# Window attention, forward and backward: the y products ahead of the first window pair, and the weight gradient row between the pairs in 64x64 products

## The chip, the cores and the metric

One core of a Trainium2 chip runs the whole program. The metric is the device time of one execution in microseconds (us). Engines are named as in the profile: PE is TensorE (matmuls; PEld is its loading of stationary operands), DVE is VectorE, ACT is ScalarE, POOL is GpSimd, and SP is SyncE, which here only starts DMAs. PSUM, where matmuls leave their sums, has eight banks.

## The reference

Attention in windows of 8x8 tokens over an image of 256x256 tokens with 384 channels, without heads. The kernel computes the output and the gradients of `x`, `wqkv` and `wo` for a given `grad_out`, all in bfloat16.

```python
xw = x in windows: (1024, 64, 384)
q, k, v = split(xw @ wqkv, 3)
p = softmax((q @ k.T) * C ** -0.5)
o = (p @ v) @ wo
# outputs: o, and of sum(o * grad_out) the gradients by x, wqkv and wo
```

## The kernel before

The kernel never forms q, k and v. It folds the weights once at the start: `A` is Wq Wk^T with the scale, `B` is Wv Wo. With x and g (the rows of `grad_out`) of a window, the scores are x A x^T, the output is P (x B), and the gradient of P is (g B^T) x^T. The gradient by x is P^T (g B^T) + dS^T (x A) + dS (x A^T). For the weights it is enough to sum two 384x384 matrices over all windows, x^T (dS x) and x^T (P^T g); the code calls dS x `Uq`, P^T g `Wq`, and the two sums `GF_acc`. The gradients of the weights come from these sums at the very end (`weight_gradients`).

**Tiles.** Two windows that lie under each other make a tile of 128 tokens, one window in partitions 0 to 63 (`LO`), the other in 64 to 127 (`HI`). Four such tiles are a quad, and 128 quads are the image. A loop handles one quad a step, in a software pipeline of three stages: in step i the quad i+1 is in stage A, quad i in stage B and quad i-1 in stage C.

**Stages.** Stage A is two projections of 3 row blocks each (`project`, L149): kind 0 makes z = B g^T, kind 1 makes y = A^T x^T, nine products of 512 columns each; ACT evicts them to `yz` (L159, L161). `gather` (L163), on DVE, copies z or y once more into `zy`, which a transposing DMA on SP's queue turns into `tok` (`to_tokens`, L169). Stage B makes the scores and the gradient of P (`scores`), the softmax and its backward in six pieces on DVE and ACT (`soft`), and x B and x A^T (`uv`, L227: eight banks, evicted by ACT at L235). Stage C is `attend` (L249), once for the tiles 0 and 1, and once for 2 and 3: a pair. Between them, and ahead of the first, `filler` (L326) takes work from `gf_group` (L311).

**attend.** All its products are 64x64: one window's 64 tokens are the rows, and the stationary operand has 64 columns. A slot (L257) is four such products with 384 moving columns: a straight one for each half, which leaves its result in its own half of the partitions, and a crossed one for each half, which leaves it in the other half. A pair is six slots. It uses eight PSUM tiles: two `pw`, two `pu`, two `po` (one each per token tile, straight) and two `pd` (crossed, accumulated over the slots). In the order in which they are first written: slot 1 takes `pw` and both `pd`, slot 2 `pw`, slot 3 `pu`, slot 4 `po`, slot 5 `pu`, slot 6 `po`. Slot by slot they are evicted: `pw` of the first tile by ACT (L281), `pw` of the second by DVE (L283), both `pu` by DVE (L285, L289), both `po` by ACT (L270), the first `pd` by ACT (L270), the second in halves (L296 on ACT, L297 on DVE for the first pair and on ACT for the second). Then POOL starts the stores (L298 to L305).

**gf_group.** When three quads are finished, their contribution to `GF_acc` is added: two matrices (f) of three row blocks (ma) make six rows. A row is twelve full 128x128 products (3 quads times 4 tiles) that accumulate in one PSUM tile `pg` (L320), and one DVE addition into `GF_acc` (L321). `filler(1)` makes one row; it is called twice in a step.

**Order.** The order of each engine's instructions is the order of the calls; nothing is reordered. All PSUM tiles come from one ring of eight banks, in the order of their first writes: a tile gets the bank whose last reader stands earliest, and PE waits for that reader. In the allocation of the kernel before, for instance, slot 6 of the first pair gets the bank of the `pg` ahead of it. One step (L334) allots 33 tiles: 1 for the scores, 8 for `uv`, 3 for z, 1 `pg`, 8 for the first pair, 3 for y, 1 `pg`, 8 for the second pair. On PE a step is therefore: scores, `uv`, z, row, pair, y, row, pair. On DVE, from the first row on: the addition, L283, L285, L289, L297, gather of z, gather of y, the addition, L283, L285, L289. On ACT: z, pair, y, pair. On SP's queue, in order: the turns of g and x for the quad after next (`load_turn`, L129), the turn of P and dS (`turn`), four loads of x, the turn of `zy`.

Of the kernel before, what the change touches and what calls it, by code (L numbers as in the profile page):

```python
# [9 lines left out]
ALU = mybir.AluOpType  # L10
AX = mybir.AxisListType
BF16 = mybir.dt.bfloat16
F32 = mybir.dt.float32

P = 128
WIN = 8
WT = WIN * WIN
QUAD = 4
# [4 lines left out]
def kernel(  # L23
# [21 lines left out]
    nc = tc.nc  # L45
    _, H, W, C = x.shape
# [10 lines left out]
    ring = ctx.enter_context(tc.tile_pool(name="ring", bufs=8, space=bass.MemoryType.PSUM))  # L57
# [11 lines left out]
    GF_acc = const.tile([P, 2, CK, C], F32)  # L69
# [41 lines left out]
    def weight_rest():  # L111
        weight_product(B_sb, wT[2], wo_sb, None)
        weight_product(AT_sb, wT[1], wT[0], scale)

    def windows(ap, st, first, count=2):
        row, col = st["at"]
        return ap[0, row + WIN * first:row + WIN * (first + count), col:col + WIN, :]

    LO, HI = slice(0, WT), slice(WT, P)
    OTHER = {0: HI, WT: LO}  # L120

    def load(st):
        st["xq"] = xq = grp.tile([P, QUAD, C], BF16, tag="xq", name="xq", bufs=2 * GQ + 4)
        st["dq"] = dq = qp.tile([P, QUAD, C], BF16, tag="dq", name="dq", bufs=6)
        for t in range(QUAD):
            nc.sync.dma_start(out=xq[:, t, :], in_=windows(x, st, 2 * t))
            nc.gpsimd.dma_start(out=dq[:, t, :], in_=windows(grad_out, st, 2 * t))  # L127
# [16 lines left out]
    def product(out, lhsT, rhs, start, stop):  # L144
        nc.tensor.matmul(out, lhsT=lhsT, rhs=rhs, start=start, stop=stop)  # L145
# [37 lines left out]
    def over_k(ap, n=P):  # L183
        return ap.unsqueeze(2).broadcast_to([n, QUAD, WT])

    def soft(st, step):
        sd = st["sd"]
        if step == 0:
# [53 lines left out]
    def operand(st, n, t, h):  # L242
        if n in ("PT", "ST"):
            return st["PS"][h, t, int((n == "ST") == (h == LO)), :]
        if n in ("z", "y"):
            return st["tok"][h, int(n == "y"), :, t, :]
        return st[n][h, t, :]

    def attend(st, pair):  # L249
        if pair[0] == 0:  # L250
            st["Uq"] = grp.tile([P, QUAD, C], BF16, tag="Uq", name="Uq")
            st["Wq"] = grp.tile([P, QUAD, C], BF16, tag="Wq", name="Wq")

        def bank(name):
            return ring.tile([P, C], F32, tag="r", name=name)

        def slot(straight, crossed, start=False, stop=False):  # L257
            for h in (LO, HI):
                dst, lhs, rhs, t = straight
                products = [(h, dst[h, :], lhs, rhs, t, {"start": True, "stop": True})]  # L260
                lhs, rhs, t = crossed
                o = OTHER[h.start]
                dst = pd[int((t == t0) == (h == LO))]
                products.append((o, dst[o, :], lhs, rhs, t, {"start": start, "stop": stop}))
                for o, dst, lhs, rhs, t, flags in products if h == LO else products[::-1]:
                    nc.tensor.matmul(dst, lhsT=operand(st, lhs, t, h), rhs=operand(st, rhs, t, h), **flags)  # L266

        def keep(name, src):
            sb = ob.tile([P, C], BF16, tag=name, name=name)
            nc.scalar.copy(out=sb[:], in_=src[:])  # L270
            return sb

        t0, t1 = pair
        pw = {t: bank("pw") for t in pair}
        pu = {t0: bank("pu")}
        pd = [bank("pd") for outer in (0, 1)]
        po = {t0: bank("po")}
        pu[t1] = bank("pu")
        po[t1] = bank("po")
        slot((pw[t0], "Pb", "dq", t0), ("Pb", "z", t0), start=True)  # L280
        nc.scalar.copy(out=st["Wq"][:, t0, :], in_=pw[t0][:])  # L281
        slot((pw[t1], "Pb", "dq", t1), ("dS", "y", t0))
        nc.vector.tensor_copy(out=st["Wq"][:, t1, :], in_=pw[t1][:])  # L283
        slot((pu[t0], "ST", "xq", t0), ("Pb", "z", t1), start=True)
        nc.vector.tensor_copy(out=st["Uq"][:, t0, :], in_=pu[t0][:])  # L285
        slot((po[t0], "PT", "uq", t0), ("dS", "y", t1))
        o0 = keep("o", po[t0])
        slot((pu[t1], "ST", "xq", t1), ("ST", "vq", t0), stop=True)
        nc.vector.tensor_copy(out=st["Uq"][:, t1, :], in_=pu[t1][:])  # L289
        slot((po[t1], "PT", "uq", t1), ("ST", "vq", t1), stop=True)  # L290
        o1 = keep("o", po[t1])
        inner = keep("d", pd[0])
        if t0 == 0:
            st["mid"], st["rim"] = [ob.tile([P, C], BF16, tag="d", name="d") for k in range(2)]
        upper, lower = (st["rim"], st["mid"]) if t0 == 0 else (st["mid"], st["rim"])
        nc.scalar.copy(out=lower[LO, :], in_=pd[1][LO, :])  # L296
        (nc.scalar.copy if t0 else nc.vector.tensor_copy)(out=upper[HI, :], in_=pd[1][HI, :])  # L297
        nc.gpsimd.dma_start(out=windows(out_0, st, 2 * t0), in_=o0[:])  # L298
        nc.gpsimd.dma_start(out=windows(out_0, st, 2 * t1), in_=o1[:])
        nc.gpsimd.dma_start(out=windows(out_1, st, 2 * t0 + 1), in_=inner[:])  # L300
        if t0 == 0:
            nc.gpsimd.dma_start(out=windows(out_1, st, 0, 1), in_=st["rim"][HI, :])
        else:
            nc.gpsimd.dma_start(out=windows(out_1, st, 3), in_=st["mid"][:])
            nc.gpsimd.dma_start(out=windows(out_1, st, 7, 1), in_=st["rim"][LO, :])  # L305

    fill = []

    final = {}

    def gf_group(sts, last=False):  # L311
        n = len(sts) * QUAD
        for f in range(2):
            if last:
                final[f] = grp.tile([P, CK, C], BF16, tag="Uq", name="GFb")
            for ma in range(CK):
                pw = ring.tile([P, C], F32, tag="r", name="pg")
                for i in range(n):
                    st, t = sts[i // QUAD], i % QUAD
                    product(pw[:], st["xq"][:, t, ma * P:(ma + 1) * P], st["UW"[f] + "q"][:, t, :], i == 0, i == n - 1)  # L320
                nc.vector.tensor_tensor(out=GF_acc[:, f, ma, :], in0=pw[:], in1=GF_acc[:, f, ma, :], op=ALU.add)  # L321
                if last:
                    nc.vector.tensor_copy(out=final[f][:, ma, :], in_=GF_acc[:, f, ma, :])
                yield

    def filler(n):  # L326
        while n and fill:
            try:
                next(fill[0])
                n -= 1  # L330
            except StopIteration:
                fill.pop(0)

    def step(c, b, a, ahead):  # L334


        def on(st):
            return (lambda f, *r: f(st, *r)) if st is not None else (lambda f, *r: None)
        C_, B, A = on(c), on(b), on(a)
        B(scores)  # L340
        B(soft, 0)
        if b is not None and c is None:
            weight_rest()
        B(uv, 0, 0)
        B(uv, 0, 1)
        B(soft, 1)
        B(uv, 1, 0)
        B(uv, 1, 1)
        B(soft, 2)
        B(soft, 3)  # L350
        B(uv, 2, 0)
        B(uv, 2, 1)
        B(uv, 3, 0)
        B(uv, 3, 1)
        B(soft, 4)
        for mo in range(CK):
            A(project, 0, mo)
        B(soft, 5)
        B(turn)
        if ahead is not None:  # L360
            load(ahead)
        filler(1)
        C_(attend, (0, 1))
        A(gather, 0)
        for mo in range(CK):
            A(project, 1, mo)
        A(gather, 1)
        A(to_tokens)
        filler(1)
        C_(attend, (2, 3))  # L370

    G_ON_PE, X_ON_PE = 4, 1
    EV = {"z": "AAA", "y": "AAA", "u": "AAAA", "v": "AAAA", "o": "AAAA", "U": "DDDD", "W": "DDDD", "d": "AAAA"}
    quads = [(row, col) for row in range(0, H, 2 * WIN * QUAD) for col in range(0, W, WIN)]
    sts = [{"at": q, "i": i} for i, q in enumerate(quads)]
    n = len(sts)
# [41 lines left out]
    with tc.manual_schedule(engines=MANUAL):  # L418
# [19 lines left out]
        for i in range(-1, n + 1):  # L438
            if 0 <= i < n - 2:
                load_turn(sts[i + 2])  # L440
            step(get(i - 1), get(i), get(i + 1), get(i + AHEAD) if i >= 0 else None)
            if 0 < i + 2 < G_ON_PE:
                turn_on_pe(sts[i + 2], "dq", "dT")
            if i == 1:
                turn_blocks(woT_sb, wo_sb)
            if i > 0:
                held.append(sts[i - 1])
                sts[i - 1] = None
            if held and i == n:
                last = gf_group(held, True)  # L450
            elif len(held) == GQ:
                fill.append(gf_group(held))
                held = []
        filler(1 << 30)
        weight_gradients(last)

# [29 lines left out]
```

## Time and profile before

| | us |
|---|---|
| median of 3 runs | 1943.18 |
| lowest, highest | 1942.42, 1948.91 |
| the profiled execution (span) | 1942.8 |
| PE busy | 1926.6 |
| ACT busy | 1546.3 |
| DVE busy | 1458.9 |
| POOL busy | 895.2 |

A line of the groups or of a timeline names the source line, the engine, the operation, the tiles written and read, the shape, and how many instructions it stands for; in a timeline the first two numbers are the start and the time until the last of them ended. In brackets stands how long the engine had been idle before, and what it waited for. Consecutive instructions on one engine overlap a little, so their durations can add up to more than the time that they took together: twelve products of 384 columns have 326 ns each, and take 2.11 us. Durations of one, in ns: a 128x128 product with 384 columns 326, a 64x64 one 318 to 348, the addition into `GF_acc` 558, a cast of 384 columns out of PSUM 548 on DVE and 473 to 500 on ACT, an eviction of z or y 607 to 644, a `gather` copy 560.

### The profile page before, as it was taken

How to read it: one execution, taken by the hardware profiler on the slowest of the kernel's cores; microseconds unless marked ns; L12 is line 12 of the kernel's file. 1: busy time of each engine (PE TensorE's matmuls, PEld its weight loads, DVE VectorE, ACT ScalarE, POOL GpSimd, SP SyncE). 2: the span in 40 equal slices, each digit the busy share in tenths (PEclk: the TensorE clock that was granted, in tenths of full speed). 3: DMA queues.
4: the chain of work that ended last, by engine and by line, in shares of the span. 5: the costliest groups of instructions: out<-in, count | busy, mean ns of one | idle time of the engine just before them, and what ended most of it. 6: DMA issues, size and time to landing. Idle time of an engine off the chain costs nothing.

```text
span 1942.8 us, 48771 instructions
## 1 busy us (share of the span) xinstructions
PE 1926.6 (99%) x17859; PEld 1076.9 (55%) x17859; DVE 1458.9 (75%) x3244; ACT 1546.3 (80%) x3613; POOL 895.2 (46%) x1670
## 2 busy tenths in 40 slices
PE   9999999999999999999999999999999999999999
PEld 5555555555555555555555555555555555555555
DVE  6777767777777777777777777777777777777776
ACT  7878878778777878887787878788887878887775
POOL 3445444444444445444444454454444445444432
PEclk9999999999999999999999999999999999999999
DMA  8999999999999999999999999999999999999994
GB/s 186 220 222 227 224 204 222 224 217 224 223 221 226 226 220 223 226 221 220 219 228 222 221 219 229 221 225 217 230 218 228 224 219 220 226 224 219 222 195 109
DMA packets 1017584, 423.21 MB, mean 218 GB/s; under 512 B 899584, under 2 KB 992768, under 8 KB 1017344
## 3 DMA queue, kind: packets, MB, share of 16 engines
q1 hardware_dynamic: 935984, 267.85, 79.0%
q0 software_dynamic: 79872, 151.17, 30.8%
q8 instruction: 140, 2.29, 0.5%
q10 hardware_dynamic: 1488, 1.08, 0.2%
q14 instruction: 100, 0.82, 0.1%
HBM read 101.84 MB, written 101.84 MB: 105 GB/s over the span
## 4 chain that ended last, share of the span: by engine, by line
PE 94%; ACT 2%; DMA 2%; DVE 1%; issue 0%; SPq 0%; POOL 0%; ACTq 0%; POOLq 0%
PE pj L145 49%; PE pg L145 25%; PE pw L266 6%; PE sd L145 5%; PE pu L266 4%; PE po L266 4%; DMA PS<-ps 1%; DMA dT<-dq 1%; PE pd L266 1%; ACT uq L235 0%; ACT vq L235 0%; DMA dq<-in_grad_out_dram 0%; ACT yz L159 0%; PE pe L385 0%; SPq L134 0%
## 5 line engine op out<-in xcount | busy, mean ns | idle before, releaser
L298 POOL DMA_DIRECT2D out_dram<-o x256 | 137.7, 538 | 936.8 <-ACT o L270 915.8
L145 PEld LDWEIGHTS <-xq 128*128 128x128 bf16 x3072 | 300.0, 98 | 226.4 <-issue 2.0
L145 PEld LDWEIGHTS <-xT 128*128 128x128 bf16 x3072 | 291.6, 98 | 182.7
L145 PE MATMUL pj<-B_sb,xT 128*128 128x384 bf16 x1536 | 333.5, 326 | 0.0
L145 PE MATMUL pj<-AT_sb,xT 128*128 128x384 bf16 x1536 | 333.3, 326 | 0.0
L127 POOL DMA_DIRECT2D dq<-in_grad_out_dram x512 | 271.9, 547 | 40.4 <-DMA out_dram<-o 17.6
L281 ACT CAST Wq<-pw 128x384 bf16<-128x384 f32 x256 | 123.0, 480 | 200.1 <-PE pw L266 200.0
L145 PE MATMUL pj<-dT,BT_sb 128*128 128x512 bf16 x1152 | 271.3, 381 | 5.1 <-DMA dT<-dq 5.1
L145 PE MATMUL pg<-Uq,xq 128*128 128x384 bf16 x1536 | 270.4, 326 | 0.5 <-DVE GF_acc L321 0.5
L145 PE MATMUL pj<-xT,A_sb 128*128 128x512 bf16 x1152 | 270.8, 380 | 0.0
L145 PE MATMUL pg<-Wq,xq 128*128 128x384 bf16 x1536 | 270.4, 326 | 0.0
L321 DVE TENSOR_TENSOR GF_acc<-pg,GF_acc 128x384 f32<-128x384 f32 x258 | 143.9, 558 | 152.8 <-PE pg L145 152.7
L235 ACT CAST uq<-pj 128x384 bf16<-128x384 f32 x512 | 249.9, 488 | 7.3 <-PE pj L145 1.0
L235 ACT CAST vq<-pj 128x384 bf16<-128x384 f32 x512 | 255.1, 498 | 0.1
L270 ACT CAST o<-po 128x384 bf16<-128x384 f32 x512 | 220.9, 484 | 5.1 <-PE po L266 2.4
L211 ACT COPY ps<-Pb 64x256 bf16<-64x256 bf16 x256 | 103.2, 403 | 149.7 <-DVE Pb L208 148.2
L159 ACT CAST yz<-pj 128x512 bf16<-128x512 f32 x384 | 206.7, 644 | 2.1 <-PE pj L145 2.0
L161 ACT CAST yz<-pj 128x512 bf16<-128x512 f32 x384 | 200.8, 607 | 0.2
L145 PEld LDWEIGHTS <-BT_sb 128*128 128x128 bf16 x1152 | 112.4, 98 | 129.8 <-DMA dT<-dq 7.0
L145 PEld LDWEIGHTS <-A_sb 128*128 128x128 bf16 x1152 | 102.3, 98 | 139.9 <-issue 33.6
L167 DVE COPY zy<-yz 128x1536 bf16<-128x1536 bf16 x256 | 143.4, 560 | 46.3 <-ACT yz L161 39.8
L266 PE MATMUL pd<-tok,Pb 64*64 64x384 bf16 x1024 | 173.3, 335 | 0.0
(89 smaller groups left out, 3376.1 us busy)
## 6 DMA issues: line engine op xcount, KB each, us to landing
xq<-in_x_dram SPq DMA_DIRECT2D x512, 96.0 KB, 4.2
dq<-in_grad_out_dram POOLq DMA_DIRECT2D x512, 96.0 KB, 4.0
out_dram<-o POOLq DMA_DIRECT2D x512, 96.0 KB, 4.0
out_dram<-d POOLq DMA_DIRECT2D x384, 96.0 KB, 4.2
out_dram<-d POOLq DMA_DIRECT2D x256, 48.0 KB, 4.3
tok<-zy SPq DMA_TRANSPOSE x128, 7.6
PS<-ps SPq DMA_TRANSPOSE x128, 4.7
xT<-xq SPq DMA_TRANSPOSE x127, 6.3
```

What stands on the lines that cost most here:

```text
L127: nc.gpsimd.dma_start(out=dq[:, t, :], in_=windows(grad_out, st, 2 * t))
L145: nc.tensor.matmul(out, lhsT=lhsT, rhs=rhs, start=start, stop=stop)
L159: ENG[EV["z"][mo]](out=yz[:, mo, :, 0:4:3, :], in_=pj[:])
L161: ENG[EV["y"][mo]](out=yz[:, mo, :, 1:3, :], in_=pj[:])
L167: nc.vector.tensor_copy(out=st["zy"][:, kind, :, :, :, :], in_=src)
L211: nc.scalar.copy(out=ps[h, :, w, :], in_=Pb[h, :, :])
L235: cp(out=dst[:, t, :], in_=pj[:])
L266: nc.tensor.matmul(dst, lhsT=operand(st, lhs, t, h), rhs=operand(st, rhs, t, h), **flags)
L270: nc.scalar.copy(out=sb[:], in_=src[:])
L281: nc.scalar.copy(out=st["Wq"][:, t0, :], in_=pw[t0][:])
L298: nc.gpsimd.dma_start(out=windows(out_0, st, 2 * t0), in_=o0[:])
L321: nc.vector.tensor_tensor(out=GF_acc[:, f, ma, :], in0=pw[:], in1=GF_acc[:, f, ma, :], op=ALU.add)
```

## The change

Three edits. First, in `step`, the four calls that make y (with both gathers and `to_tokens`) move ahead of the first pair, and the first `filler(1)` goes behind them. PE's order becomes: scores, `uv`, z, y, row, pair, row, pair. On DVE both gathers then stand ahead of the first row's addition and of the first pair's casts; on ACT the y evictions stand directly behind those of z. Second, the row between the pairs (in steps that have a quad in stage C) is made by `gf_rows_tiled`: in place of a 128x128 product four 64x64 ones, two for each half of the tokens, each into its own half of the output's rows. The straight ones accumulate in one bank, the crossed ones in another, and DVE adds both to `GF_acc`, one after the other. A step thus allots 34 PSUM tiles. Third, for the second pair the cast of the second `pw` (L283) goes from DVE to ACT.

```diff
-        nc.vector.tensor_copy(out=st["Wq"][:, t1, :], in_=pw[t1][:])
+        (nc.scalar.copy if t0 else nc.vector.tensor_copy)(out=st["Wq"][:, t1, :], in_=pw[t1][:])
...
+    def gf_rows(sts, f, ma):
+        pw = ring.tile([P, C], F32, tag="r", name="pg")
+        n = len(sts) * QUAD
+        for i in range(n):
+            st, t = sts[i // QUAD], i % QUAD
+            product(pw[:], st["xq"][:, t, ma * P:(ma + 1) * P], st["UW"[f] + "q"][:, t, :], i == 0, i == n - 1)
+        return [pw]
+
+    def gf_rows_tiled(sts, f, ma):
+        straight, crossed = [ring.tile([P, C], F32, tag="r", name="pg") for k in range(2)]
+        n = len(sts) * QUAD
+        for i in range(n):
+            st, t = sts[i // QUAD], i % QUAD
+            for h in (LO, HI):
+                products = ((h, straight), (OTHER[h.start], crossed))
+                for o, dst in products if h == LO else products[::-1]:
+                    nc.tensor.matmul(dst[o, :], lhsT=st["xq"][h, t, ma * P + o.start:ma * P + o.stop],
+                                     rhs=st["UW"[f] + "q"][h, t, :], start=(i == 0), stop=(i == n - 1))
+        return [straight, crossed]
+
     def gf_group(sts, last=False):
-        n = len(sts) * QUAD
...
-                pw = ring.tile([P, C], F32, tag="r", name="pg")
-                for i in range(n):
-                    st, t = sts[i // QUAD], i % QUAD
-                    product(pw[:], st["xq"][:, t, ma * P:(ma + 1) * P], st["UW"[f] + "q"][:, t, :], i == 0, i == n - 1)
-                nc.vector.tensor_tensor(out=GF_acc[:, f, ma, :], in0=pw[:], in1=GF_acc[:, f, ma, :], op=ALU.add)
+                for pw in (gf_rows_tiled if tiled[0] else gf_rows)(sts, f, ma):
+                    nc.vector.tensor_tensor(out=GF_acc[:, f, ma, :], in0=pw[:], in1=GF_acc[:, f, ma, :], op=ALU.add)
...
-    def filler(n):
+    def filler(n, in_tiles=False):
+        tiled[0] = in_tiles
...
-        filler(1)
-        C_(attend, (0, 1))
         A(gather, 0)
         for mo in range(CK):
             A(project, 1, mo)
         A(gather, 1)
         A(to_tokens)
         filler(1)
+        C_(attend, (0, 1))
+        filler(1, c is not None)
         C_(attend, (2, 3))
```

More of the change, by code (lines that the diff above doesn't have):

```diff
@@ L307 @@
     fill = []
+    tiled = [False]
     final = {}
+    def gf_rows(sts, f, ma):
[16 more added lines that the diff above has]
+        return [straight, crossed]
     def gf_group(sts, last=False):
-        n = len(sts) * QUAD
         for f in range(2):
```

## The prediction

> **What bounds the kernel now.** I read the head of the page and its chain first, then the timeline of one step in the middle of the run, then the groups by shape for the mean durations.
>
> ```profile
> PE 1926.6 (99%) x17859; PEld 1076.9 (55%) x17859; DVE 1458.9 (75%) x3244; ACT 1546.3 (80%) x3613; POOL 895.2 (46%) x1670
> ...
> PE 94%; ACT 2%; DMA 2%; DVE 1%; issue 0%; SPq 0%; POOL 0%; ACTq 0%; POOLq 0%
> ```
>
> PE is the chain: nearly nothing ever makes it wait. So a step costs what PE's instructions cost, plus what the other engines newly make PE wait. In the trace the steps start (first `sd` product to first `sd` product) 14.80 us apart, almost without scatter. One step, in parts (the columns: start, duration, engine, line, operation):
>
> ```profile
> 1001.05 2.11 PE L145 MATMUL pg<-Wq,xq 128*128 128x384 bf16 x12
> 1003.10 0.35 PE L266 MATMUL pw<-dq,Pb 64*64 64x384 bf16 x1
> ...
> 1003.45 0.32 PE L266 MATMUL pu<-xq,PS 64*64 64x384 bf16 x1
> ...
> 1003.61 0.32 PE L266 MATMUL po<-uq,PS 64*64 64x384 bf16 x1
> ...
> 1003.94 0.32 PE L266 MATMUL po<-uq,PS 64*64 64x384 bf16 x1
> ...
> 1004.20 2.12 PE L145 MATMUL pj<-xT,A_sb 128*128 128x512 bf16 x9
> ```
>
> What to see: a slot of four 64x64 products starts every 0.16 us (1003.45, 1003.61), which is also what one 128x128 product takes (12 in 2.11, the last 0.33 long: 0.162 each). At the borders between the two shapes there is more: the last `pg` product starts at 1002.83 and the first slot 0.27 later instead of 0.16; that slot takes 0.18 to 0.19 instead of 0.16; and the last slot starts at 1003.94 and `pj` 0.26 later. Going in and out costs 0.10 + 0.02 + 0.10 = 0.22 us, twice in a step.
>
> ```profile
> 1008.30 0.56 DVE L321 TENSOR_TENSOR GF_acc<-pg,GF_acc 128x384 f32<-128x384 f32 x1 [0.67 <-PE pg L145]
> ...
> 1008.78 0.55 DVE L283 CAST Wq<-pw 128x384 bf16<-128x384 f32 x1
> ...
> 1009.03 0.32 PE L266 MATMUL po<-uq,PS 64*64 64x384 bf16 x1
> ...
> 1009.09 0.86 ACT L270 CAST o<-po 128x384 bf16<-128x384 f32 x2
> ...
> 1009.30 0.87 PE L145 MATMUL sd<-xT,yz 128*128 128x64 bf16 x24
> ...
> 1016.75 1.61 ACT L159 CAST yz<-pj 128x512 bf16<-128x512 f32 x3
> ```
>
> What to see here: the bank of `pg` is read by VectorE until 1008.86, and the sixth slot, which needs the last of the eight banks, starts at 1009.03. All eight banks are claimed by the eight tiles of a pair, and the margin is 0.17 us. And ScalarE evicts the `z` products, which PE began at 1013.91, only from 1016.75: it is late there because its `uq` and `vq` casts wait for the softmax chain.
>
> ```profile
> 1005.48 1.56 ACT L161 CAST yz<-pj 128x512 bf16<-128x512 f32 x3
> ...
> 1007.07 0.56 DVE L167 COPY zy<-yz 128x1536 bf16<-128x1536 bf16 x1 [0.30 <-ACT yz L161]
> ```
>
> The second `gather` copy waits for the last `y` eviction, and starts 0.03 after it.
>
> **The change, part by part**, in us per step; it acts on 125 steps (42 groups of six rows are drained two per step, from the fifth step with a finished quad on; the two left over are made at the end, untiled).
>
> *Switches, -0.22.* With `y` ahead of the pair and the row between the pairs in 64x64 shape, PE goes into that shape and out of it once in a step instead of twice. Nothing else changes in PE's work: twelve 128x128 products of 0.162 become twelve slots of four 64x64 products at 0.162, 1.95 us both times. No row shows twelve such slots in a sequence into two banks; the nearest is the pair itself, whose later slots keep 0.16 with accumulating and overwriting products mixed. I take that value. Bounds: no gain, since no row shows 384 columns in less than 0.16, and +1.95 if the slots ran at half the rate (two pairs of products after each other).
>
> The Trainium skill (TensorE: Matmul & The Clock Gate, section LDWEIGHTS) gives a weight load its column count over 1.2 GHz, and four loads of 64 columns would then be 213 ns in a slot, above 162. By that rule the twelve slots would take 2.56 us, some 76 us more in the run. The pair's slots start four loads of 107 ns each and still come every 162 ns, so here the row decides.
>
> *Banks of the second pair, +0.55.* I put zero at the first product of the second pair (1008.19 now). A pair takes eight banks; six come from the first pair, and the two that are left are those of the tiled row, since the pair's own first bank is read until 0.89 (1008.60 plus 0.48, less 1008.19). The last tiled slot starts at -0.16 and its products end at 0.16; VectorE starts 0.04 later (1008.30 now, after an end of 1008.26) and adds for 0.56, to 0.76; slot 5 wants that bank at 0.65 and gets it at 0.79. The second add reads and writes the same slice of `GF_acc`; I let it start as dependent VectorE work does in the trace, 0.03 after the end: 0.79 to 1.35. Slot 6 starts at 1.38 instead of 0.84. The scores start 0.27 later, at 1.65 (now 1.10): +0.55. If the second add overlaps the first as L283 does L321 (0.48 apart, 1008.30 and 1008.78) this is 0.43; with hand-overs to PE of 0.07, 0.62. The L283 cast that goes to ScalarE (0.37 apart in a run of such casts) is free there: the second `o` cast behind it waits for slot 6 anyway. If slot 6 weren't late, that queue would be 0.37 later.
>
> *VectorE behind the gather, +0.24.* The second `o` cast, now at 1.27, starts at 1.76, and all that ScalarE does behind it, up to the `z` evictions, is 0.49 later: 9.05 instead of 8.56. The `y` evictions no longer stand behind the first pair's casts but directly behind the `z` ones: three casts 0.48 apart put them at 10.50, and 1.56 more ends them at 12.06. The gather waits for this, 12.09 to 12.65, and on VectorE the add of the first `pg` row and the L283 cast now stand behind the gather: the add runs from 12.68 to 13.24. PE meanwhile: scores 1.65, `z` 4.62 later, `y` 1.95, `pg` 1.95, and in at 12.20 (1.95 + 0.09 on); slot 6 would start at 13.03, and needs the bank of `pg`: 13.27. Bounds: 0, if ScalarE comes 0.25 earlier; 0.45, if it comes that much later.
>
> *The bank of the crossed products, +0.31.* The tiled row is next, at 13.43. Its straight bank is that of the first `pw` (read to 13.1 by ScalarE), its crossed one that of the second `pw`, whose cast (L283) starts 0.48 behind the add, at 13.16, and ends at 13.71: 13.74. Were VectorE not late at all, the cast would still end 1.13 after the pair began, as it does now (1003.68 + 0.55 - 1003.10), and the row wants the bank at 1.00: the low end is 0.15, the high one 0.40. Twelve slots later, at 15.69, the second pair begins; now it is 14.80.
>
> *Queues.* SP issues the same in the same order: the turn of `zy` stays behind the loads, and is some 7 us late already (issued at 1014.97 for a gather that ended at 1007.63). The `xT` turn issued at 1007.33 lands 6.3 later, at 1013.6; the `y` products that read it start 9.7 after the scores now (1019.0), 6.6 then (1015.9). So 2.3 us are left; in the steps where SP is later than this PE would wait, as now for `dT` (the groups show 5.1 us on PE and 7.0 on its weight loads in the whole run): 0 to 12, taken as 0. POOL's order stays; its stores follow the casts.
>
> Sum: -0.22 + 0.55 + 0.24 + 0.31 = 0.88; times 125, 110. The profiled execution spans 1942.8, so 2053; the median of the runs, 1943.18, is 0.4 above that span, which I leave out.
>
> **The rivals.**
> *Only the waits that the number of banks forces* (chance 0.15): the adds overlap, ScalarE is early enough for the gather: 0.43 + 0.15 - 0.22 = 0.36, times 125: 1988. For it: 0.24 hangs on ScalarE's lateness, which I carried over eight microseconds. Against: the `o` cast is tied to slot 6.
> *The switches alone* (0.05): the banks come free in time, 127 steps gain 0.22: 1915. This needs the sixth slot of the second pair served by 0.81, that is both adds over within 0.65 of the row's end, where with the hand-over two take 1.1 to 1.2 by the rows. It decides only if banks are handed out otherwise than I think. Somewhere between, within 0.3%: 0.03.
> *Half rate in the tiled row* (0.05): 1.95 more in each step on top of the forecast, 244: 2297. For it speaks that both banks take products from both row halves at once. Against it: so does the bank of `pw`, `pu` and `po` now, at full rate.
> The Trainium skill (TensorEngine Tiling, Gotcha 1) says that different row tiles can't access one bank at the same time, which taken literally would be this rival. The pair's slots show no such cost where the halves go to different partitions.
>
> **How the numbers follow.** The forecast, bank waits with a late VectorE, has 0.72, and gives 2053. The low end is the first rival's 1988; the high end takes the upper bounds, 0.62 + 0.45 + 0.40 - 0.22 = 1.25 or 156: 2099, of which I keep 2090, since all of them together are unlikely. 0.3% is 6 us, about what a measurement of this kernel can tell from no change. Slower: 0.72 + 0.15 + 0.05 = 0.92; same 0.03; faster 0.05.
>
> **What the profile after would show.** PE's share falls to some 94%, with idle time before `pu` and `po` of the second pair put down to VectorE's adds (L321's successor), before `po` of the first pair put down to the same line, and before the first crossed product put down to L283. Steps 15.5 to 15.8 apart. One PE weight-load gap of 0.3 (into the shape) in a step instead of two. Tiled slots 0.16 apart. It would be wrong if PE showed no idle time at the sixth slot, or if tiled slots were more than 0.2 apart.

## The result and the profile after

The changed kernel takes 2040.38 us (median of 4, 2034.85 to 2042.81) where the kernel before takes 1942.80: slower by the factor 1.0497 (95% interval 1.0471 to 1.0522). The profiled execution spans 2041.0, 98.2 more than that of before. In the trace the steps are 15.545 us apart (median over 100 steps, first scores product to first scores product) where they were 14.796. 0.749 more, times the 123 steps from the fifth on, is 92 of the 98 us; most of the rest is in steps that wait for a transfer.

The head of the page after and its chain:

```profile
span 2041.0 us, 58149 instructions
...
PE 1979.9 (97%) x22359; PEld 1164.0 (57%) x22359; DVE 1469.2 (72%) x3241; ACT 1605.5 (79%) x3741; POOL 893.6 (44%) x1670
...
ACT 44%; PE 19%; issue 12%; DVE 11%; DMA 9%; POOL 3%; SPq 0%; POOLq 0%; ACTq 0%
```

The busy share of PE hardly moved, from 99% to 97%, and would mislead. The chain tells it: before, 94% of the way back from the end went over PE; now 44% of it goes over ScalarE's casts, 11% over VectorE (the gather and the addition among others) and 19% over PE. PE's share stays high because a product is recorded as 0.32 us long where the next could have started after 0.16, so the first 0.16 of every wait hides under the product ahead of it (the 0.46 below is recorded as 0.28 idle).

One step of the changed kernel, in its timeline (start, duration, engine, line, operation; idle time before and its releaser in brackets). First, what happens around the first pair:

```profile
960.15 1.65 ACT L161 CAST yz<-pj 128x512 bf16<-128x512 f32 x3
...
961.83 0.56 DVE L167 COPY zy<-yz 128x1536 bf16<-128x1536 bf16 x1 [0.91 <-ACT yz L161]
...
962.42 0.32 PE L266 MATMUL pu<-xq,PS 64*64 64x384 bf16 x1
...
962.42 0.56 DVE L338 TENSOR_TENSOR GF_acc<-pg,GF_acc 128x384 f32<-128x384 f32 x1
...
962.90 0.55 DVE L283 CAST Wq<-pw 128x384 bf16<-128x384 f32 x1
963.04 0.32 PE L266 MATMUL po<-uq,PS 64*64 64x384 bf16 x1 [0.28 <-DVE GF_acc L338]
...
963.20 2.44 PE L328 MATMUL pg<-Wq,xq 64*64 64x384 bf16 x48
```

The `y` evictions end at 961.80, the gather follows at 961.83, the addition at 962.42, done at 962.98, and only at 963.04 can the sixth slot (`po`) start, 0.62 after the fifth where 0.16 would do: 0.46 lost. The addition itself could have started at 961.85, just after its products ended (961.81). In the kernel before it did start that early, 0.10 after the first product of its pair (1003.10):

```profile
1003.20 0.56 DVE L321 TENSOR_TENSOR GF_acc<-pg,GF_acc 128x384 f32<-128x384 f32 x1 [0.46 <-PE pg L145]
```

In the changed kernel the 48 products of the 64x64 row take 2.44 instead of the 2.1 of twelve slots: they begin at 963.20 on the straight bank, and the second of them, on the crossed bank, starts only at 963.50, behind the L283 cast that ends at 963.45. That is another 0.30. Then the second pair:

```profile
965.68 1.15 DVE L338 TENSOR_TENSOR GF_acc<-pg,GF_acc 128x384 f32<-128x384 f32 x2 [0.43 <-PE pg L328]
...
965.81 0.32 PE L266 MATMUL po<-uq,PS 64*64 64x384 bf16 x1
965.84 0.48 ACT L281 CAST Wq<-pw 128x384 bf16<-128x384 f32 x1 [1.18 <-PE pw L266]
...
965.97 0.32 PE L266 MATMUL po<-uq,PS 64*64 64x384 bf16 x1
...
966.29 0.32 PE L266 MATMUL pu<-xq,PS 64*64 64x384 bf16 x1
...
966.46 0.32 PE L266 MATMUL po<-uq,PS 64*64 64x384 bf16 x1
...
966.76 0.86 PE L145 MATMUL sd<-xT,yz 128*128 128x64 bf16 x24
```

The first of the two additions runs from 965.68 to 966.24, and `pu` of slot 5 starts at 966.29, 0.32 after the last product of slot 4 (965.97): 0.17 lost. `po` of slot 6 then starts 0.16 later, while the second addition, which ends at 966.83, is still running. It waits for nothing.

So, against the step before: -0.22 for the changes of shape, +0.46, +0.30 and +0.17 for three waits. That makes 0.71 of the 0.749; most of the rest is some 0.02 to 0.03 each time that PE starts again after a wait, when three of the four products of the first slot are recorded with 0.35 and the slot takes 0.18 to 0.19.

### The profile page after: what moved, and what is told of

Its sections match the earlier page's. It is cut to its first block, busy times and chain, and to the rows that moved or that the text cites. A ratio compares the mean times of both kernels' runs of the same rounds, so it can differ in the third digit from the quotient of the medians.

```text
span 2041.0 us, 58149 instructions
## 1 busy us (share of the span) xinstructions
PE 1979.9 (97%) x22359; PEld 1164.0 (57%) x22359; DVE 1469.2 (72%) x3241; ACT 1605.5 (79%) x3741; POOL 893.6 (44%) x1670
## 4 chain that ended last, share of the span: by engine, by line
ACT 44%; PE 19%; issue 12%; DVE 11%; DMA 9%; POOL 3%; SPq 0%; POOLq 0%; ACTq 0%
PE pg L328 11%; ACT vq L235 8%; ACT yz L161 7%; ACT yz L159 7%; ACT uq L235 7%; ACT o L270 4%; DMA xT<-xq 3%; DVE GF_acc L338 3%; DVE zy L167 3%; ACT d L297 2%; DVE Pb L208 2%; DVE rs L204 2%; ACT ps L211 2%; ACT ex L200 2%; PE pj L145 2%
## 5 line engine op out<-in xcount | busy, mean ns | idle before, releaser
L338 DVE TENSOR_TENSOR GF_acc<-pg,GF_acc 128x384 f32<-128x384 f32 x383 | 213.6, 558 | 73.5 <-PE pg L328 52.1
L270 ACT CAST o<-po 128x384 bf16<-128x384 f32 x512 | 234.3, 493 | 36.9 <-PE po L266 33.6
L328 PEld LDWEIGHTS <-xq 64*64 64x64 bf16 x6000 | 213.4, 106 | 63.5 <-issue 38.4
L266 PE MATMUL po<-uq,PS 64*64 64x384 bf16 x1024 | 194.9, 325 | 32.6 <-DVE GF_acc L338 31.6
L145 PEld LDWEIGHTS <-xq 128*128 128x128 bf16 x1572 | 153.6, 98 | 114.9 <-issue 0.5
L161 ACT CAST yz<-pj 128x512 bf16<-128x512 f32 x384 | 211.6, 673 | 3.6 <-PE pj L145 2.7
L266 PEld LDWEIGHTS <-PS 64*64 64x64 bf16 x3072 | 138.2, 105 | 130.1 <-issue 107.1
L159 ACT CAST yz<-pj 128x512 bf16<-128x512 f32 x384 | 206.0, 640 | 0.3 <-PE pj L145 0.2
L328 PE MATMUL pg<-Wq,xq 64*64 64x384 bf16 x3984 | 202.0, 324 | 0.0
L145 PEld LDWEIGHTS <-A_sb 128*128 128x128 bf16 x1152 | 111.7, 98 | 149.6 <-DVE ps L223 6.5
```

Of the source, the lines that this page charges most:

```text
L159: ENG[EV["z"][mo]](out=yz[:, mo, :, 0:4:3, :], in_=pj[:])
L161: ENG[EV["y"][mo]](out=yz[:, mo, :, 1:3, :], in_=pj[:])
L328: nc.tensor.matmul(dst[o, :], lhsT=st["xq"][h, t, ma * P + o.start:ma * P + o.stop], rhs=st["UW"[f] + "q"][h, t, :], start=(i == 0), stop= ...
```

## The experiments

All runs at a glance. The period and the waits are medians over 100 steps of each run's trace; "lengthened" is the sum of what single steps took above the period, most of it waits for the turns of g and x; the last column is the ratio to runs of the kernel before that were taken beside it, with its 95% interval.

| kernel | us | period | slot 6, first pair | banks of the second row | slot 5, second pair | lengthened | ratio |
|---|---|---|---|---|---|---|---|
| before | 1942.8 | 14.796 | 0 | 0 | 0 | 10 | |
| changed | 2040.4 | 15.545 | 0.46 | 0.30 | 0.17 | 14 | 1.0497 (1.0471 to 1.0522) |
| y ahead only | 1997.2 | 15.217 | 0.40 | 0 | 0 | 9 | 1.0294 (1.0270 to 1.0319) |
| 64x64 row only | 1967.6 | 15.004 | 0 | 0 | 0.18 | 3 | 1.0135 (1.0110 to 1.0160) |
| first row ahead of y | 2036.2 | 15.590 | 0 | 0.81 | 0.17 | 6 | 1.0492 (1.0470 to 1.0515) |
| that, gather late | 1990.8 | 14.971 | 0 | 0.18 | 0.17 | 38 | 1.0251 (1.0227 to 1.0275) |
| changed, short second addition | 2041.3 | 15.542 | 0.46 | 0.30 | 0.17 | 12 | 1.0506 (1.0467 to 1.0544) |
| changed, cast back on VectorE | 2029.0 | 15.425 | 0.21 | 0.30 | 0.17 | 21 | 1.0449 (1.0416 to 1.0483) |
| changed, gather late | 1995.1 | 14.968 | 0 | 0.18 | 0.17 | 45 | 1.0271 (1.0228 to 1.0315) |
| that, crossed one slot behind | 1990.8 | 15.003 | 0 | 0.02 | 0 | 28 | 1.0273 (1.0210 to 1.0336) |
| y ahead, gather late, plain rows | 1983.3 | 14.797 | 0 | 0 | 0 | 46 | 1.0202 (1.0163 to 1.0241) |

**The two halves of the change, each alone.** First the y products ahead of the first pair with both rows as before:

```diff
-        (nc.scalar.copy if t0 else nc.vector.tensor_copy)(out=st["Wq"][:, t1, :], in_=pw[t1][:])
+        nc.vector.tensor_copy(out=st["Wq"][:, t1, :], in_=pw[t1][:])
...
-        filler(1, c is not None)
+        filler(1)
```

> The y products ahead of the first pair, everything else as before: both rows in 128x128 shape, the cast of the second pair's second pw on VectorE. Theory (PE waits for PSUM banks): PE goes in and out of the 64x64 shape twice, so nothing is saved; the bank of the first row is freed behind the gather of y, which ends some 2.6 us after the y products, so slot 6 of the first pair waits about 0.4 us a step; no other wait. 1943 + 127 x 0.4 = about 1993 us. Rival (the 64x64 row with its second addition is what costs): about 1943. Rival (it is the 0.46 at slot 6 that is small and the rest elsewhere): under 1960.

1997.2 us, close to the theory's 1993. The wait is where it was expected, and there is no other at a bank; the sixth slot in the timeline of this run:

```profile
1014.49 0.32 PE L266 MATMUL pu<-xq,PS 64*64 64x384 bf16 x1
1015.04 0.32 PE L266 MATMUL po<-uq,PS 64*64 64x384 bf16 x1 [0.23 <-DVE GF_acc L338]
```

0.55 apart instead of 0.16. Then the 64x64 row (and the cast on ScalarE) with y where it was:

```diff
+        filler(1)
+        C_(attend, (0, 1))
         A(gather, 0)
...
         A(to_tokens)
-        filler(1)
-        C_(attend, (0, 1))
         filler(1, c is not None)
         C_(attend, (2, 3))
```

> The second row made of 64x64 products in two banks, and the cast moved to ScalarE, but the y products where they were, between the first pair and that row. Theory: the number of changes of shape is that of before, so nothing is saved; the crossed bank has long been free; slot 5 of the second pair waits about 0.17 us for the first of the two additions. 1943 + 125 x 0.17 to 0.22 = 1964 to 1971 us. Rival (the 64x64 row itself costs): about as slow as the whole change, 2030 to 2040. Rival (slot 6 waits for the second addition too, as predicted): 0.55 a step, 2012.

1967.6 us, within the expected range. This rules the products of the row out as the cause: its twelve slots in two banks cost what twelve full products cost. In its timeline:

```profile
1015.84 2.15 PE L328 MATMUL pg<-Wq,xq 64*64 64x384 bf16 x48
...
1018.03 1.15 DVE L338 TENSOR_TENSOR GF_acc<-pg,GF_acc 128x384 f32<-128x384 f32 x2 [0.81 <-PE pg L328]
...
1018.31 0.32 PE L266 MATMUL po<-uq,PS 64*64 64x384 bf16 x1
...
1018.64 0.32 PE L266 MATMUL pu<-xq,PS 64*64 64x384 bf16 x1
```

48 products in 2.15, where twelve full ones take 2.11. Slot 5 (`pu` at 1018.64) waits for the first addition, which ends 0.56 after 1018.03; it comes 0.33 behind slot 4 in place of 0.16. Alone, the two halves cost 0.42 and 0.21 a step. Together they cost 0.75, although only together do they save the 0.22 of the changes of shape, which is seen as the missing gap between row and pair (965.32 in the changed kernel is 0.16 behind the row's last straight product in its half of the array). Added up, 0.42 and 0.21 less 0.22 would be 0.41; most of what is new in the combination is the wait for the crossed bank (0.30), which neither has alone.

**The prediction's step that was too large.** I had slot 6 of the second pair wait for the second addition. To see what that addition costs I cut it to 8 columns, so that this kernel leaves the rest of the crossed products out of the weight gradients.

```diff
-                for pw in (gf_rows_tiled if tiled[0] else gf_rows)(sts, f, ma):
-                    nc.vector.tensor_tensor(out=GF_acc[:, f, ma, :], in0=pw[:], in1=GF_acc[:, f, ma, :], op=ALU.add)
+                for k, pw in enumerate((gf_rows_tiled if tiled[0] else gf_rows)(sts, f, ma)):
+                    cols = slice(0, 8 if k else C)
+                    nc.vector.tensor_tensor(out=GF_acc[:, f, ma, cols], in0=pw[:, cols], in1=GF_acc[:, f, ma, cols], op=ALU.add)
```

> The changed kernel, but the addition of the crossed bank into GF_acc takes 8 of its 384 columns (the rest of the crossed products is left out of the weight gradients). The banks go to the same tiles. The prediction's step (slot 6 of the second pair waits for the second addition, 0.41 us a step): 50 us less than the changed kernel, about 1990 us. Reading of the trace (slot 6 gets the bank of its own pair's first pw, free by then, so only the first addition is waited for): the second addition costs next to nothing, only the softmax starts some 0.05 us earlier behind the Uq casts; 2030 to 2040 us.

2041.3 us and a period of 15.542: no difference. The second addition is hidden: in the changed kernel's timeline above it ends at 966.83, when slot 6 (966.46) and the scores (966.76) have both started. In the program slot 6 has the bank of its own pair's first `pw`, which ScalarE has read by 966.32 in the timeline above (965.84 plus 0.48), ahead of the 966.46 at which slot 6 starts.

**The first row ahead of y.** If the addition stands behind the gather only because the row stands behind y, the row can go first.

```diff
+        filler(1)
         A(gather, 0)
...
         A(to_tokens)
-        filler(1)
         C_(attend, (0, 1))
```

> The changed kernel, but the first row stands ahead of the y products, not behind them: order z, row, y, pair, 64x64 row, pair. Its addition on VectorE then comes before both gathers. Theory: the 0.46 us of slot 6 of the first pair goes; the cast that frees the crossed bank still stands behind the gather of y and that wait stays at 0.27; slot 5 of the second pair 0.17; changes of shape -0.22: +0.22 a step, about 1971 us. Rival (ScalarE with one cast more and late y evictions sets the pace): not below 2020.

2036.2 us: the theory's 1971 failed, and the rival's bound held. The wait at slot 6 did go, but the row's waits grew from 0.30 to 0.81. Its timeline shows why:

```profile
1002.85 2.10 PE L145 MATMUL pj<-xT,A_sb 128*128 128x512 bf16 x9
...
1003.70 1.88 ACT L161 CAST yz<-pj 128x512 bf16<-128x512 f32 x3 [0.22 <-PE pj L145]
...
1005.61 0.56 DVE L167 COPY zy<-yz 128x1536 bf16<-128x1536 bf16 x1 [1.53 <-ACT yz L161]
...
1006.01 0.32 PE L328 MATMUL pg<-Wq,xq 64*64 64x384 bf16 x1
...
1006.09 0.55 DVE L283 CAST Wq<-pw 128x384 bf16<-128x384 f32 x1
...
1006.69 2.14 PE L328 MATMUL pg<-Wq,xq 64*64 64x384 bf16 x47 [0.36 <-DVE Wq L283]
```

With the row first, PE makes y two microseconds later, directly ahead of the pair. The `y` evictions now wait for PE, one by one, and end at 1005.58; the gather and behind it the L283 cast are later still, against a pair that starts no later (1004.89). I had taken the eviction's end from the changed kernel, where ScalarE set it. ScalarE's pace, the rival's reason, isn't what sets it here: its first eviction waits 0.22 for PE, and the two others follow at PE's pace.

**The gather behind the casts.** Both kernels, with the first row ahead of y and behind it, got the gather of y moved on VectorE to behind the first pair's `Uq` casts:

```diff
-        A(gather, 1)
-        A(to_tokens)
+        def late():
+            A(gather, 1)
+            A(to_tokens)
...
-        C_(attend, (0, 1))
+        C_(attend, (0, 1), late)
...
+        between()
         inner = keep("d", pd[0])
```

With the row ahead of y:

> As the run with the row ahead of y, and the gather of y on VectorE goes behind the first pair's Uq casts, ahead of the cast of the last half bank. Theory: the cast that frees the crossed bank starts as soon as its slot is over and ends 1.10 to 1.15 after the pair began, where the row wants the bank at 1.00: 0.16; slot 5 of the second pair 0.17; -0.22: +0.11 a step, about 1957 us. Rival (the gather, now later, holds up the additions of the 64x64 row): as without it, 1971 or more.

And with the row behind y, as in the change:

> The changed kernel, only the gather of y (with the turn of zy behind it) goes behind the first pair's Uq casts on VectorE; the first row stays behind the y products. Theory: the first addition starts 0.12 after the pair began, as before the change; slot 6 of the first pair doesn't wait (0.62 now), the crossed bank is free about 1.18 after the pair began, 0.2 late; slot 5 of the second pair 0.17; -0.22: a period of 14.95 us. By that alone 1962 us. The run with the row ahead of y and the late gather had 28 us more than its period explains, in steps that waited for the dT and xT turns; if it is the late turn of zy or the shorter period that brings these, this kernel has them too: 1985 to 1990 us. Rival (ScalarE sets the pace): a period above 15.4.

Periods of 14.971 and 14.968, where 14.91 and 14.95 were expected: the wait at slot 6 is gone in both, and the crossed bank is left with 0.18. The second one's timeline:

```profile
1399.90 0.56 DVE L339 TENSOR_TENSOR GF_acc<-pg,GF_acc 128x384 f32<-128x384 f32 x1 [0.93 <-PE pg L145]
...
1400.37 0.55 DVE L283 CAST Wq<-pw 128x384 bf16<-128x384 f32 x1
1400.47 0.32 PE L266 MATMUL pu<-xq,PS 64*64 64x384 bf16 x1
...
1400.63 0.32 PE L266 MATMUL po<-uq,PS 64*64 64x384 bf16 x1
...
1400.79 2.33 PE L329 MATMUL pg<-Wq,xq 64*64 64x384 bf16 x48
```

VectorE now waits for PE (0.93) and not PE for it; slot 6 comes 0.16 after slot 5. The row takes 2.33 because its crossed products start after the cast ends at 1400.92. With only the gather moved, this shows that its place causes the 0.46. By the periods alone (0.17 more, times 125) both would take some 1964 us. They take 1990.8 and 1995.1; the difference is in lengthened steps, 28 and 35 us more of them than before, most of it waits for late turns. For the first I had not foreseen that, and the second is still above the 1985 to 1990 that I had put.

**What lengthens those steps.** Late gather without the 64x64 row:

```diff
-        filler(1, c is not None)
+        filler(1)
```

(on the kernel before it, and the cast back on VectorE)

> The y products ahead of the first pair with both rows in 128x128 shape (as the first experiment), and the gather of y behind the first pair's Uq casts. Theory: the 0.42 us of slot 6 comes from the gather alone, so the period is that of before, 14.80 us, and by it alone 1943. The steps lengthened by late turns: 10 us in all before, 3 with the 64x64 row alone, 38 and 45 in the two runs with y ahead and the gather late. If y ahead with the late gather brings them whatever the row's shape, here too: 1970 to 1985 us; if the 64x64 row is needed for it, 1940 to 1950.

The period is 14.797, within a nanosecond that of the kernel before: without the gather ahead of the casts, y ahead of the pair costs nothing in the steady step. But 46 us go to lengthened steps, and most of that is in these waits of PE and its weight loads:

```profile
PE pj L145 <- DMA xT<-xq: 25.6, 24, 1.9
...
PEld L145 <- DMA dT<-dq: 10.6, 10, 3.8
...
PE pj L145 <- DMA dT<-dq: 7.0, 9, 3.4
```

(us in total, times, longest.) So the row's shape isn't needed for it. Nor is it the late turn of `zy` or the shorter period alone: the kernel with only the 64x64 row has its gather at the same place in the step (12.6 us after the scores, here 12.5), a period of 15.00, and 3 us. Nor is y ahead alone enough: with the gather ahead of the casts ("y ahead only") it has 9 us. So it takes both, y ahead of the pair and the late gather. With y ahead the products read `xT` 3.1 us earlier, and the stores of both pairs stand closer together; which of the two meets the late gather, and how, wasn't separated.

**The cast that moved to ScalarE, put back.**

```diff
-        (nc.scalar.copy if t0 else nc.vector.tensor_copy)(out=st["Wq"][:, t1, :], in_=pw[t1][:])
+        nc.vector.tensor_copy(out=st["Wq"][:, t1, :], in_=pw[t1][:])
```

> The changed kernel with the cast of the second pair's second pw back on VectorE. Theory: the chain from the second pair to the y evictions runs over ScalarE, which gets 0.1 us earlier (it waits for slot 6 before its second o cast anyway), so slot 6 of the next first pair waits 0.1 less: 2025 to 2030 us. Rival (VectorE, now with five instructions in a row, starts the softmax 0.46 later and that sets the pace): the softmax's exp waits for ScalarE's casts with 0.8 us to spare, so this needs more than that; if it holds, 2060 us or more.

2029.0 us in the expected range, and the period is 0.12 shorter: in sum the third edit cost some 10 us (the intervals of the two ratios overlap a little; the periods are apart). ScalarE ends the y evictions 10.34 after the scores and not 10.59, and slot 6 of the first pair waits 0.21 instead of 0.46, where I had expected 0.1 less. But the scores now wait 0.14, which I had not expected, for the second addition: they start 0.05 after it ends.

**Can the waits be scheduled away?** On the kernel with the late gather, the crossed products one slot behind:

```diff
-        for i in range(n):
-            st, t = sts[i // QUAD], i % QUAD
-            for h in (LO, HI):
-                products = ((h, straight), (OTHER[h.start], crossed))
-                for o, dst in products if h == LO else products[::-1]:
+        for s in range(n + 1):
+            products = ((LO, LO, straight, s), (LO, HI, crossed, s - 1), (HI, LO, crossed, s - 1), (HI, HI, straight, s))
+            for h, o, dst, i in products:
+                if 0 <= i < n:
+                    st, t = sts[i // QUAD], i % QUAD
```

> As the changed kernel with the late gather, and in the 64x64 row the crossed products run one slot behind the straight ones, so the row takes thirteen slots; the straight bank is complete one slot earlier, the crossed one is wanted one slot later. Theory: the wait for the crossed bank (0.22) goes, and so does slot 5's wait for the first addition (0.17); the thirteenth slot costs 0.16, and slot 6 may wait up to 0.1 for the bank of its own pair's first pw: a period of 14.75 to 14.87 us. By the period alone 1938 to 1952 us; with the turns as late as in the run with the late gather, 40 us more. Rival (slot 5 waits for something else than the first addition): its wait stays, and the period is 14.9 or more.

Both waits went, as expected: 0.02 is left at the crossed bank, and for slot 5 the timeline shows how.

```profile
1015.45 1.22 DVE L339 TENSOR_TENSOR GF_acc<-pg,GF_acc 128x384 f32<-128x384 f32 x2
...
1015.86 0.35 PE L266 MATMUL pd<-tok,dS 64*64 64x384 bf16 x2
1016.06 0.32 PE L266 MATMUL pu<-xq,PS 64*64 64x384 bf16 x1
```

The first of the two additions ends at 1016.01 (0.56 after 1015.45) and slot 5 starts 0.05 after that, as it does in every kernel here with the 64x64 row; this is what shows that it waits for the first addition. But the addition comes a slot earlier now, and the second of slot 4's crossed products starts at 1015.89, so that slot 5 follows it at 0.17 and next to nothing is lost. Still the period is 15.003, not 14.75 to 14.87, and by the period alone the rival would have seemed right. The thirteenth slot costs 0.16, slot 6 waits 0.08, and the scores wait 0.15 for the crossed bank, which the program now hands to them, until its addition ends. That 1990.8 us is still near the expectation with late turns is luck: the period is longer and the lengthened steps weigh less (18 us more than before, not 40). In a ring of eight banks the wait moved to the next tile in line.

No version that I tried is faster than the kernel before.

## Why the prediction was right

The direction and the mechanism were right (PE waits for banks whose readers come late), and so were the places of the waits, but for one that never came. 2040.4 lies in the range 1988 to 2090, 13 us under the forecast of 2053; that it is so near is in part luck, since two terms were off in opposite directions. By its steps:

*Switches, -0.22.* Right. The row between the pairs takes 12 slots at 0.162 and no gap stands between it and the second pair. The rival of half rate is out: 2.15 us for 48 products.

*Banks of the second pair, +0.55.* Wrong in size: 0.17. The step that failed is "Slot 6 starts at 1.38 instead of 0.84". The waiting for the first addition was right (0.14 forecast), but I ruled out the pair's own first bank because it is read until 0.89, and forgot that slot 5's wait had already put slot 6 at 0.95. So slot 6 takes that bank and never meets the second addition, and the experiment with the short addition shows that it costs nothing. That both additions had to be over before slot 6 was no bound, and so the low end of 1988, which has 0.43 for this term, was none either: with the late gather PE waits 0.18 at the crossed bank and 0.17 at slot 5, and the period alone would give some 1964.

*VectorE behind the gather, +0.24.* Right in its mechanism, mis-sized: 0.46, just above the upper bound of 0.45. ScalarE's chain was forecast to end the y evictions 10.41 after the scores (12.06 less 1.65); it ended them at 10.59, as the z evictions began 7.51 after the scores and not 7.40 (9.05 less 1.65), and the y ones took 1.65 and not 1.56; PE came to the pair no later. Nor was the cast that went to ScalarE "free there": put back, it made the step 0.12 shorter. Term two and term three hang on one chain, and what isn't lost in the second pair and at the scores is partly lost here: with y ahead only, 0 there and 0.40 here; with the cast back, 0.31 there and 0.21 here. So errors of -0.38 and +0.22, with 0.04 for PE's fresh starts and -0.01 at the crossed bank, left 0.13 in the period (0.88 forecast, 0.75 measured).

*The bank of the crossed products, +0.31.* Measured 0.30.

*Queues, 0.* 4 us more in lengthened steps than before, 8 waits for `xT` among them, inside the 0 to 12. In the kernels with the late gather, lengthened steps weigh 28 to 46 us.

*What the profile would show.* The steps at 15.545 (15.5 to 15.8 forecast) are there, and so is the idle time before `po` of the first pair (0.28). `po` of the second pair doesn't wait, and the waits of its `pu` and of the first crossed product are seen only in the starts, since they leave PE hardly any idle time. PE's share was forecast at 94% and is 97%: I counted the waits in full, where the first 0.16 of each hides under the product ahead.

## What to carry to other kernels

Where every PSUM bank is in use, count for each group of products which reader must be done before it can start: what goes between two groups also gives the readers their time, and saving 0.22 us of changes of shape came with 0.9 us of waits here. When an instruction is moved, see what now stands behind it on the engine that does the reading; here one copy of 0.56 us ahead of an addition cost 0.4 us a step. And when a wait delays the next tile as well, ask again which bank is free by then, instead of adding the waits up.

## What I had not expected of the hardware

The four 64x64 quarters of the array ran as streams of their own here. Where the crossed bank came 0.30 late, the straight quarter of the first half kept its lead: the second pair's first product starts at 965.32, the same slot's last one at 965.48, and each next slot keeps the distance until a wait evens it out.
